# Attention by pairs of heads in plain fp32, in a kernel of attention and two feed-forward layers

## The chip, the cores and the metric

The kernel runs on one core of one Trainium2 chip. The number that counts is the device time of one execution, in microseconds (us): the median of three runs before the change is 675.22 us (674.95 to 675.29). Five engines work side by side, each through its own queue in a fixed order: TensorE (PE, the matmuls; PEld is its loading of stationary operands), VectorE (DVE), ScalarE (ACT), GpSimd (POOL) and SyncE (SP, which issues the transfers).

## What is computed

Attention with a window and sinks, then two feed-forward layers, on 2 x 768 = 1536 tokens, 8 heads of 64 dimensions, model width 512, hidden width 2048:

```python
scores = (q @ k.T) / sqrt(64)                  # per batch and head, 768 x 768
keep   = (col < n_sink) | ((row - col >= 0) & (row - col < window))   # n_sink 4, window 128
a      = softmax(where(keep, scores, -1e9));   x = a @ v
h = relu(x @ w_in);  y = (h * h) @ w_out       # first layer
h = y @ w_in2;  g = (a0 + a1 h + a2 h^2 + a3 h^3) / (1 + |b0||h| + |b1| h^2 + 1e-6)
out = g @ w_out2                               # second layer
```

Only scores within 128 positions, and those of the first few columns, count. So a block of 128 queries needs its own block of keys, the block before it, and the first 32 columns (the sinks).

## The kernel before, in words

**Units and groups.** The tokens are cut into four groups (`GROUPS`): group 0 has 512 tokens (two segments of two query blocks), groups 1 and 2 have 256 (one segment), group 3 has 512 (two). A unit of attention is one head of one segment, that is two query blocks: 48 units, 16 of them in segments that begin a sequence ("first" segments: their blocks need 128 and 256 key columns) and 32 in later ones ("later" segments: 288 columns for each block, previous, sinks and own). By group: 16 units (8 first, 8 later) in group 0, 8 later ones in group 1, 8 first ones in group 2, 16 later ones in group 3.

**Steps of a unit** (`att_unit`, a generator whose `yield`s are ticks): scores on PE (line 305) into a PSUM bank, mask, minimum and row statistic on DVE (309), exponential and row sum on ACT (311), reciprocal (315, 316) and normalising (318) on DVE or POOL, transposes on PE (334 for the window, 338 for the 32 sink columns), copies out of PSUM (339, 341), value matmuls on PE (359 for the sinks, 368 for the window), and the evacuation into x (376, 384 and after).

**Two ways to be exact.** The feed-forward matmuls split each fp32 operand into a high and a low part in a rounded format (fp32r) and add three products (lines 447 to 449, 470 to 474, 505 to 507). The attention does the same in "split" units: k and v are split (282, 284, 290, 291), q is stacked as high part over low part on the 128 rows (283, 285), and the probabilities are split on their way out of PSUM (339, 347, 349). In group 0, `PAT = "ppps"` makes three of four units "plain": the matmuls take fp32 operands as they are. The fourth, which is always a later one, is plain for the values and split for the scores. A plain score matmul finds k and q twice on the 128 rows, and q is scaled by half (277).

**What sets the order.** The loop before the first layer runs the 16 units of group 0, one new unit every four ticks. Then `group(g)` runs the two matmul stages of the first layer for group g, and in `slot` it lets attention ticks of the next groups in between (`NUNIT[g]` units, four ticks each). What attention of group g+1 is left at the end of group g runs alone (`while done < gdone[g + 1]`). A scheduler orders the instructions of each engine by a model of time; in groups 1 and 2 (`PINNED`) PE keeps the order of the code. Attention has PSUM banks 2, 3, 6, 7 and 1 ahead of the first layer, 6 and 7 while a group of 512 tokens is in work, and 2, 3, 6 and 7 beside a group of 256. From group 3 on no attention is left, and the second layer follows.

Of the kernel before, what the change touches and what calls it, by code (L numbers as in the profile page):

```python
# [19 lines left out]
P = 128  # L20
# [19 lines left out]
NUNIT = (8, 12, 12)  # L40
CONV = (6, 10, 14, 18, 46, 50)
PAT = "ppps"
# [10 lines left out]
ST_T = 5  # L53
ST_PV = 2
# [8 lines left out]
def seg_dims(seg):  # L63
    _, blk0, nb = seg
    pv = 1 if blk0 > 0 else 0
    wk = nb * KB + P if pv else nb * P
    wq = nb * P
    nkb = nb + pv
    wv = (nkb + pv) * D
    return wk, wq, nkb, wv  # L70


def units():
    out = []
    for g, segs in enumerate(GROUPS):
        for h in range(H):
            xo = 0
            for seg in segs:
                out.append((g, h, seg, xo))
                xo += seg[2] * P  # L80
    return out


def pack_attention(q, k, v):
    qT = q.transpose(0, 1, 3, 2)
    kT = k.transpose(0, 1, 3, 2)
    parts = []
    for g, h, seg, _ in units():
        b, blk0, nb = seg
        cols = []  # L90
        sk = kT[b, h][:, :NSK]
        if blk0 > 0:
            cols.append(kT[b, h][:, (blk0 - 1) * P : blk0 * P])
        for i in range(nb):
            if blk0 > 0:
                cols.append(sk)
            cols.append(kT[b, h][:, (blk0 + i) * P : (blk0 + i + 1) * P])
        cols.append(qT[b, h][:, blk0 * P : (blk0 + nb) * P])
        kq = np.concatenate(cols, axis=1)
        kq = np.concatenate([kq, kq], axis=0)  # L100
        p0 = blk0 - 1 if blk0 > 0 else blk0
        vs = [v[b, h][j * P : (j + 1) * P] for j in range(p0, blk0 + nb)]
        if blk0 > 0:
            vs.append(np.concatenate([v[b, h][:NSK]] * 4, axis=0))
        vv = np.concatenate(vs, axis=1)
        parts += [kq.reshape(-1), vv.reshape(-1)]
    return np.ascontiguousarray(np.concatenate(parts))
# [43 lines left out]
class Fast:  # L151
# [17 lines left out]
    def setup(self):  # L169
# [38 lines left out]
        self.m2 = c.tile([P, KB + P], F32, name="m2")  # L208
# [4 lines left out]
        v.tensor_scalar(fut, rel, 0.0, BIG, op0=ALU.is_lt, op1=ALU.mult)  # L213
        v.tensor_scalar_add(rel1, rel, 128.0)
        cur, prv = m2[:, KB : KB + P], m2[:, 0:P]
        v.tensor_scalar(cur, rel, win, BIG, op0=ALU.is_ge, op1=ALU.mult)
        v.tensor_tensor(cur, cur, fut, op=ALU.max)
        v.tensor_scalar(out, col, ns, BIG, op0=ALU.is_ge, op1=ALU.mult)
        v.tensor_tensor(m0, cur, out, op=ALU.min)
        v.tensor_scalar(prv, rel1, win, BIG, op0=ALU.is_ge, op1=ALU.mult)  # L220
        v.tensor_tensor(m1[:, 0:P], prv, out, op=ALU.min)
        v.tensor_copy(m1[:, P : 2 * P], cur)
        v.tensor_copy(m2[:, P:KB], out[:, :NSK])
        nu = sum(u[2][2] for u in units())
# [5 lines left out]
    def alt_tags(self, alt):  # L230
        if not alt:
            return [None] * 12
        c = NF - 3 * alt
        return [f"{p}{c + i}_{k}" for i in range(3) for k in range(2) for p in ("whi", "wlo")]

    def att_load(self, u, early, alt):
        nc = self.nc
        wk, wq, nkb, wv = seg_dims(u[2])
# [5 lines left out]
        rv = self.att_tile("rawv", wv, F32, bufs=2, alt=self.alt_tags(alt)[9])  # L244
        off = self.att_off
        self.att_off = off + P * (w + wv)
        a = self.io["att"]
        nc.sync.dma_start(raw, a[off : off + P * w].rearrange("(p w) -> p w", w=w))
        off += P * w
        nc.sync.dma_start(rv, a[off : off + P * wv].rearrange("(p w) -> p w", w=wv))  # L250
        return raw, rv

    def att_tile(self, tag, n, dt=F32R, bufs=1, alt=None):
        if alt:
            return self.wp.tile([P, WH], dt, tag=alt, name=tag)[:, :n]
        return self.att.tile([P, n], dt, tag=tag, name=tag, bufs=bufs)

    def att_unit(self, u, raws, alt):
        nc = self.nc
        tags = self.alt_tags(alt)  # L260
        V, A, G = nc.vector, nc.scalar, nc.gpsimd
        g, h, seg, xo = u
        mode = PAT[self.unit_i % len(PAT)] if g == 0 else "b"
        self.unit_i += 1
        plain, plain_pv = mode == "p", mode in "ps"
        b, blk0, nb = seg
        wk, wq, nkb, wv = seg_dims(seg)
        pv = nkb - nb
        n = nb * P
        at = self.att  # L270
        raw, vr = raws
        kr, qr = raw[:, :wk], raw[:, wk:]
        vr3 = vr.rearrange("p (j d) -> p j d", d=D)
        qst = self.att_tile("qst", wq, F32 if plain else F32R, alt=tags[2])
        if plain:
            ks = [kr]
            V.tensor_scalar_mul(qst, qr, -0.0625)
        else:
            khi = self.att_tile("khi", wk, alt=tags[0])
            klo = self.att_tile("klo", wk, alt=tags[1])  # L280
            ks = [khi, klo]
            V.tensor_copy(khi, kr)
            A.mul(qst, qr, -0.125)
            G.tensor_tensor(klo, kr, khi.bitcast(F32), op=ALU.subtract)  # L284
            V.scalar_tensor_tensor(qst[64:128], in0=qr[64:128], scalar=-0.125,
                                   in1=qst[64:128].bitcast(F32), op0=ALU.mult, op1=ALU.subtract)
        yield
        if not plain_pv:
            vst = self.att_tile("vst", (nkb + pv) * 2 * D, alt=tags[3]).rearrange("p (j d) -> p j d", d=2 * D)
            A.copy(vst[:, :, 0:D], vr3)  # L290
            G.tensor_tensor(vst[:, :, D : 2 * D], vr3, vst[:, :, 0:D].bitcast(F32), op=ALU.subtract)
        yield
        ps, sums = [], self.const.tile([P, 4], F32, tag="sums", name="sums", bufs=6)
        for i in range(nb):
            blk = blk0 + i
            if pv:
                off, w, m = i * KB, KB + P, self.m2
# [4 lines left out]
            sc = self.att_bank()  # L302
            ql = qst[:, i * P : (i + 1) * P]
            for j, kk in enumerate(ks):
                nc.tensor.matmul(sc[:, :w], ql, kk[:, off : off + w], start=(j == 0), stop=(j == len(ks) - 1))  # L305
            pt = self.att_tile("p", KB + P, F32, bufs=4, alt=tags[4 + i])
            mn = self.mn[:, self.mn_i : self.mn_i + 1]
            self.mn_i += 1
            self.lastV = V.tensor_tensor_reduce(pt[:, :w], sc[:, :w], m, scale=1.0, scalar=3.0e38,  # L309
                                                op0=ALU.add, op1=ALU.min, accum_out=mn)  # L310
            self.lastA = A.activation(pt[:, :w], pt[:, :w], AF.Exp, scale=-1.0, bias=mn,  # L311
                         accum_out=sums[:, i : i + 1])
            ps.append((pt, w, blk))
            yield
        V.tensor_scalar_add(sums[:, :nb], sums[:, :nb], 1e-9)
        V.reciprocal(sums[:, :nb], sums[:, :nb])
        for i, (pt, w, blk) in enumerate(ps):
            (G if g in NORM_POOL else V).tensor_scalar(pt[:, :w], pt[:, :w], sums[:, i : i + 1], 0.0,
                                               op0=ALU.mult, op1=ALU.add)
# [683 lines left out]
```

## Time and profile before

| | us |
|---|---|
| median of 3 runs | 675.22 |
| the profiled execution | 675.02 |
| its span, first to last instruction | 673.2 |
| PE busy in the span | 648.8 |
| DVE busy | 509.0 |
| ACT busy | 475.3 |
| POOL busy | 163.5 |

A matmul's record lasts longer than its turn on PE: records overlap, and the next one starts while the one before it is still leaving the array. What a matmul costs is therefore the distance from its start to the next start, read from a timeline, and not the length of its record. Another habit of the records: a plain fp32 matmul has two records of equal shape, an fp32r matmul and a transpose have one.

### The profile page before, as it was taken

Reading aid. Unit: us, or ns where it says so; the run is one execution under the profiler, and the core shown is the slowest. Engines: PE = TensorE matmul, PEld = TensorE weight load, DVE = VectorE, ACT = ScalarE, POOL = GpSimd, SP = SyncE. Lnnn points to the kernel's source line nnn. Section 1 sums busy time; section 2 is a strip of 40 time slices with the busy share of each in tenths; the row PEclk is TensorE's granted clock in tenths of the full one; section 3 lists DMA queues with packets and bytes.
Section 4 is the critical chain, followed back from the end, with each engine's and each line's share of the span. In section 5 each row is a group of like instructions: output and inputs, shape, how many; then the busy total and the mean of one; then the engine's idle time right before and its main releaser. Section 6 shows DMA issues by size and latency. Waiting matters only on the chain.

```text
span 673.2 us, 10158 instructions
## 1 busy us (share of the span) xinstructions
PE 648.8 (96%) x3433; PEld 543.9 (81%) x3433; DVE 509.0 (76%) x1068; ACT 475.3 (71%) x1044; POOL 163.5 (24%) x174
## 2 busy tenths in 40 slices
PE   5999999999799999999999999999999999999995
PEld 3666788788699999999888888888888888888884
DVE  6976877778678877875666648999788878787772
ACT  4877977777677776776777757878677666666662
POOL 3553111111223332322100001344223333222221
PEclk9999999999799999999999999999999999999998
DMA  7761555555323222210466640000010000000001
GB/s 283 251 204 47 182 173 168 152 174 157 115 88 90 65 85 85 66 36 1 129 190 193 201 132 1 0 1 0 1 56 8 1 0 1 31 32 1 0 1 68
DMA packets 25403, 58.41 MB, mean 87 GB/s; under 512 B 3200, under 2 KB 9600, under 8 KB 25344
## 3 DMA queue, kind: packets, MB, share of 16 engines
q1 hardware_dynamic: 24768, 57.55, 26.9%
q8 instruction: 29, 0.48, 0.3%
q14 instruction: 30, 0.25, 0.1%
q10 hardware_dynamic: 576, 0.14, 0.1%
HBM read 54.53 MB, written 3.15 MB: 86 GB/s over the span
## 4 chain that ended last, share of the span: by engine, by line
PE 72%; DVE 0%; ACT 0%; issue 0%
PE b L447 11%; PE b L449 11%; PE b L448 11%; PE b L505 6%; PE b L507 6%; PE b L506 6%; PE b L470 4%; PE b L474 4%; PE b L471 4%; PE b L368 3%; PE b L305 2%; PE b L334 1%; PE b L359 1%; PE b L338 1%; PE b L658 0%
## 5 line engine op out<-in xcount | busy, mean ns | idle before, releaser
L447 PE MATMUL b<-xhi,whi 128*128 128x512 f32 (+1 forms) x320 | 111.5, 353 | 1.1 <-ACT xhi L376 0.8
L448 PE MATMUL b<-xlo,whi 128*128 128x512 f32 (+1 forms) x320 | 111.9, 350 | 0.0
L449 PE MATMUL b<-xhi,wlo 128*128 128x512 f32 (+1 forms) x320 | 111.6, 349 | 0.1
L496 POOL TENSOR_TENSOR glo<-t,ghi 128x512 fp32r<-128x512 f32 x34 | 45.0, 1323 | 213.5 <-ACT ghi L495 195.4
L470 PE MATMUL b<-ghi,whi 128*128 128x512 f32 (+1 forms) x256 | 77.0, 341 | 0.4 <-ACT b L458 0.4
L471 PE MATMUL b<-ghi,wlo 128*128 128x512 f32 (+1 forms) x256 | 76.1, 337 | 0.1
L506 PE MATMUL b<-wlo,ghi 128*128 128x512 f32 x192 | 74.7, 389 | 0.0
L505 PE MATMUL b<-whi,ghi 128*128 128x512 f32 x192 | 74.4, 389 | 0.0
L507 PE MATMUL b<-whi,glo 128*128 128x512 f32 x192 | 71.9, 389 | 0.0
L447 PEld LDWEIGHTS b<-xhi,whi 128*128 128x128 f32 x320 | 60.7, 191 | 8.5 <-ACT xhi L376 1.0
L449 PEld LDWEIGHTS b<-xhi,wlo 128*128 128x128 f32 x320 | 61.0, 191 | 8.0 <-DVE wlo L432 0.5
L448 PEld LDWEIGHTS b<-xlo,whi 128*128 128x128 f32 x320 | 61.0, 191 | 7.3
L284 POOL TENSOR_TENSOR klo<-raw,khi 128x448 fp32r<-128x448 f32 (+1 forms) x32 | 33.4, 1045 | 126.6 <-PE b L305 111.5
L311 ACT ACTIVATE p<-p,mn 128x288 f32<-128x288 f32 (+2 forms) x96 | 48.3, 503 | 19.1 <-DVE mn L309 18.6
L432 DVE TENSOR_TENSOR wlo<-wt,whi 128x512 fp32r<-128x512 f32 x64 | 44.8, 700 | 22.3 <-ACT whi L431 21.9
L431 ACT CAST whi<-wt 128x512 fp32r<-128x512 f32 x64 | 39.5, 617 | 26.9 <-PE b L448 21.0
L474 PE MATMUL b<-glo,whi 128*128 128x512 f32 (+1 forms) x256 | 56.2, 337 | 0.2 <-DVE glo L459 0.2
L309 DVE CUSTOM_DVE_ANT_0 p<-b,m 128x288 f32<-128x288 f32 (+2 forms) x96 | 39.7, 419 | 20.8 <-PE b L305 19.7
L129 DVE SCALAR_TENSOR_TENSOR wt<-st,top 128x512 int32<-128x512 int32 x64 | 48.1, 752 | 6.5 <-ACT top L128 4.4
L471 PEld LDWEIGHTS b<-ghi,wlo 128*128 128x128 f32 x256 | 48.0, 189 | 5.1 <-DVE wlo L432 0.5
L470 PEld LDWEIGHTS b<-ghi,whi 128*128 128x128 f32 x256 | 47.8, 189 | 5.1 <-ACT b L458 0.6
L128 ACT CAST top<-st 128x512 f16<-128x512 bf16 x64 | 49.6, 775 | 1.2 <-DVE wt L129 1.1
(151 smaller groups left out, 1549.3 us busy)
## 6 DMA issues: line engine op xcount, KB each, us to landing
st<-w SPq DMA_DIRECT2D x64, 512.0 KB, 3.9
raw<-att SPq DMA_DIRECT2D x24, 352.0 KB, 2.9
rawv<-att SPq DMA_DIRECT2D x32, 128.0 KB, 2.3
raw<-att SPq DMA_DIRECT2D x12, 256.0 KB, 3.5
raw_e<-att SPq DMA_DIRECT2D x8, 352.0 KB, 5.3
out<-o SPq DMA_DIRECT2D x8, 256.0 KB, 2.3
rawv<-att SPq DMA_DIRECT2D x16, 64.0 KB, 2.6
raw_e<-att SPq DMA_DIRECT2D x4, 256.0 KB, 5.5
```

Of the source, the lines that this page charges most:

```text
L128: nc.scalar.copy(top.bitcast(F16).rearrange("p (n w) -> p n w", w=2)[:, :, 1], head)
L129: nc.vector.scalar_tensor_tensor(t.bitcast(I32), in0=mid, scalar=13, in1=top, op0=ALU.logical_shift_right, op1=ALU.bitwise_or)
L311: self.lastA = A.activation(pt[:, :w], pt[:, :w], AF.Exp, scale=-1.0, bias=mn, accum_out=sums[:, i : i + 1])
L447: nc.tensor.matmul(h[:, :n], whi[:, cs], xhi[:, c, :n], start=(c == 0), stop=False)
L448: nc.tensor.matmul(h[:, :n], whi[:, cs], xlo[:, c, :n], start=False, stop=False)
L449: nc.tensor.matmul(h[:, :n], wlo[:, cs], xhi[:, c, :n], start=False, stop=(c == NC - 1))
L470: nc.tensor.matmul(acc[m], whi[:, ms], ghi, start=(f == 0 and not pk), stop=pk, **kw)
L471: nc.tensor.matmul(acc[m], wlo[:, ms], ghi, start=False, stop=pk, **kw)
L474: nc.tensor.matmul(acc[m], whi[:, ms], glo, start=False, stop=pk or f == NF - 1, **kw)
L505: nc.tensor.matmul(acc[t], ghi[:, ts_], whi, start=(f == 0), stop=False)
L506: nc.tensor.matmul(acc[t], ghi[:, ts_], wlo, start=False, stop=False)
L507: nc.tensor.matmul(acc[t], glo[:, ts_], whi, start=False, stop=(f == NF - 1))
```

## The change

A unit becomes a pair of heads of one segment, 24 units in place of 48, and all of it is plain fp32. The loads bring k and q of the first head on partitions 0 to 63 and of the second on 64 to 127, without doubling, so a score matmul of one head uses 64 of the 128 rows of the array, and the two heads write two PSUM banks. The scale goes into the mask step. No operand of the attention is split or scaled any more: lines 277, 282 to 285, 290, 291, 347 and 349 have no successor. The window's probabilities are transposed as before, one bank for each head; one goes out by ACT, the other by DVE. The sinks of both blocks (64 columns that lie side by side) are transposed by a plain fp32 matmul against the identity, 64 columns wide, each head into its half of the partitions of one bank. The value matmuls are 64 columns wide, one head on either column half of the array, and both heads leave in one copy of 128 partitions; the sinks' values come as a third load, laid out with zeros around them, so that one moving operand serves both heads. Half of the normalising of every unit (block 0) is POOL's. A unit has seven ticks instead of ten (in group 0: of fourteen), and still a new one starts every four; the ticks at which the first weights are converted, and the units per group, are halved with the units.

In the diff the lines taken out of `att_unit` are left away, as are the masks (sign turned), the packing on the host, the loads and the second program for other inputs.

```diff
 PINNED = (1, 2)
-NUNIT = (8, 12, 12)
-CONV = (6, 10, 14, 18, 46, 50)
-PAT = "ppps"
+NUNIT = (4, 4, 8)
+CONV = (3, 7, 11, 15, 23, 27)
+PER = 4
...
-ST_T = 5
-ST_PV = 2
+ST_T = 1
+ST_PV = 1
...
 def seg_dims(seg):
     _, blk0, nb = seg
     pv = 1 if blk0 > 0 else 0
-    wk = nb * KB + P if pv else nb * P
+    wk = 2 * nb * P + NSK if pv else nb * P
     wq = nb * P
     nkb = nb + pv
-    wv = (nkb + pv) * D
-    return wk, wq, nkb, wv
+    return wk, wq, nkb, nkb * P, (2 * nb * D if pv else 0)
...
     def att_unit(self, u, raws, alt):
         nc = self.nc
         tags = self.alt_tags(alt)
         V, A, G = nc.vector, nc.scalar, nc.gpsimd
...
+        g, c, seg, xo = u
         b, blk0, nb = seg
...
+        wk, wq, nkb, wv, wsk = seg_dims(seg)
         pv = nkb - nb
         n = nb * P
...
+        raw, vr = raws[:2]
         kr, qr = raw[:, :wk], raw[:, wk:]
...
+        rows = [slice(D * k, D * k + D) for k in range(2)]
+        wp_ = KB + P
+        pt = self.att.tile([P, 2, nb, wp_], F32, tag="p", name="p", bufs=2)
+        sums = self.const.tile([P, 4], F32, tag="sums", name="sums", bufs=6)
+        ws = []
         for i in range(nb):
             blk = blk0 + i
             if pv:
...
+                off, w, m = 2 * i * P, KB + P, self.m2[:, (1 - i) * NSK :][:, : KB + P]
             elif i == 0:
                 off, w, m = 0, P, self.m0
             else:
                 off, w, m = (i - 1) * P, 2 * P, self.m1
...
+            ws.append(w)
+            sc = [self.att_bank() for _ in range(2)]
+            for k, r in enumerate(rows):
+                nc.tensor.matmul(sc[k][:, :w], qr[r, i * P : (i + 1) * P], kr[r, off : off + w],
+                                 start=True, stop=True)
+            for k in range(2):
+                mn = self.mn[:, self.mn_i : self.mn_i + 1]
+                self.mn_i += 1
+                p = pt[:, k, i, :w]
+                self.lastV = V.tensor_tensor_reduce(p, sc[k][:, :w], m, scale=-0.125, scalar=3.0e38,
+                                                    op0=ALU.add, op1=ALU.min, accum_out=mn)
+                self.lastA = A.activation(p, p, AF.Exp, scale=-1.0, bias=mn,
+                                          accum_out=sums[:, k * nb + i : k * nb + i + 1])
             yield
...
+        V.tensor_scalar_add(sums[:, : 2 * nb], sums[:, : 2 * nb], 1e-9)
+        V.reciprocal(sums[:, : 2 * nb], sums[:, : 2 * nb])
+        for i in range(nb):
+            for k in range(2):
+                p = pt[:, k, i, : ws[i]]
+                (G if i in NORM_POOL else V).tensor_scalar(p, p, sums[:, k * nb + i : k * nb + i + 1], 0.0,
+                                                           op0=ALU.mult, op1=ALU.add)
         yield
         for _ in range(ST_T if g == 0 else 1):
             yield
...
+        nk = 2 * nb - (0 if pv else 1)
+        pT = []
+        for k in range(2):
+            pieces = []
+            for i in range(nb):
+                e = ws[i] - (NSK if pv and i == 0 else 0)
+                if blk0 + i > 0:
+                    pieces.append(pt[:, k, i, e - 2 * P : e - P])
+                pieces.append(pt[:, k, i, e - P : e])
+            tb = self.att_bank()
+            for j in range(nk):
+                nc.tensor.transpose(tb[:, j * P : (j + 1) * P], pieces[j], self.ident)
+            t = self.att_tile(f"pT{k}", nk * P, alt=tags[k])
+            (A.copy if k == 0 else V.tensor_copy)(t, tb[:, : nk * P])
+            pT.append(t)
+        ob = self.att_bank()
         if pv:
...
+            for k, r in enumerate(rows):
+                both = pt[:, k].rearrange("p i w -> p (i w)")
+                nc.tensor.matmul(ob[r, n : n + P], both[:, 2 * P : 2 * KB], self.ident, start=True, stop=True,
+                                 skip_group_check=True)
+            ps = self.att_tile("pS", P, alt=tags[2])
+            A.copy(ps, ob[:, n : n + P])
         yield
         for _ in range(ST_PV):
             yield
...
+        vr3 = vr.rearrange("p (j d) -> p j d", d=D)
+        o = [ob[r, :n] for r in rows]
+        if pv:
+            sv = raws[2].rearrange("p (j d) -> p j d", d=D)
+            for i in range(nb):
+                for k in range(2):
+                    nc.tensor.matmul(o[k][:, i * P : (i + 1) * P], sv[:, k * nb + i], ps,
+                                     start=i == 0, stop=False, skip_group_check=True)
         jobs, pos = [], 0
         if pv:
...
             jobs.append((0, 0, 1, 0))
             pos = 1
         for i in range(nb):
             wdt = 2 if i + 1 < nb else 1
             jobs.append((i + pv, pos, wdt, i))
             pos += wdt
...
+        for j, (vi, pp, wdt, qi) in enumerate(jobs):
+            for k in range(2):
+                nc.tensor.matmul(o[k][:, qi * P : (qi + wdt) * P], vr3[:, 2 * vi + k],
+                                 pT[k][:, pp * P : (pp + wdt) * P], start=not pv and j == 0,
+                                 stop=j == len(jobs) - 1, skip_group_check=True)
         xs = slice(xo, xo + n)
...
+        if g == 0:
             xhi, xlo = self.x[g]
...
+            A.copy(xhi[:, c, xs], ob[:, :n])
+            V.tensor_tensor(xlo[:, c, xs], ob[:, :n], xhi[:, c, xs].bitcast(F32), op=ALU.subtract)
         else:
...
+            A.copy(self.x32[g][:, c, xs], ob[:, :n])
```

The next rows are PE's order around three places, of before and of the change. In a row stand the line, the operation, what it writes and reads, and the output's size (partitions x elements); b is a PSUM bank, p the probabilities, pT their transpose.

PE beside a group of 256 tokens (group 1's matmuls), a unit of group 3 at its transposes, before:

```order
L448 MATMUL b_2983<-xlo,whi 128x256
L449 MATMUL b_2983<-xhi,wlo 128x256
L334 MATMUL b_3004<-ident,p 128x128 x4
L338 MATMUL b_3009<-ident,p 32x128 x2
L305 MATMUL b_3018<-khi,qst 128x288
L305 MATMUL b_3018<-klo,qst 128x288
L470 MATMUL b_2247<-ghi,whi 128x256
L471 MATMUL b_2247<-ghi,wlo 128x256
```

The same step of a unit of group 3 in the change, beside group 2's matmuls (L295 the scores, L327 and L335 the transposes, L427 to L429 and L450 to L454 the two stages of the first layer):

```order
L429 MATMUL b_2712<-xhi,wlo 128x256
L295 MATMUL b_2733<-raw 128x288
L295 MATMUL b_2734<-raw 128x288
L327 MATMUL b_2741<-ident,p 128x128 x4
L327 MATMUL b_2748<-ident,p 128x128 x4
L335 MATMUL b_2755<-ident,p 64x128 x2
L450 MATMUL b_2512<-ghi,whi 128x256
L451 MATMUL b_2512<-ghi,wlo 128x256
```

Transposes and scores of one head stood between full-array matmuls; now two score matmuls on 64 rows each, eight transposes and two sink matmuls of 64 columns follow each other.

PE in group 0's matmuls, the scores of one block of a later segment, before:

```order
L474 MATMUL b_1088<-glo,whi 128x512
L474 MATMUL b_1089<-glo,whi 128x512
L305 MATMUL b_1082<-khi,qst 128x288
L305 MATMUL b_1082<-klo,qst 128x288
L359 MATMUL b_1156<-pst,vst 128x256
L368 MATMUL b_1156<-pthi,vst 128x128
```

The change, the first head of a block (bank b_778), and further on the second head of it (b_779):

```order
L450 MATMUL b_804<-ghi,whi 128x512
L451 MATMUL b_804<-ghi,wlo 128x512
L295 MATMUL b_778<-raw 128x288
L454 MATMUL b_802<-glo,whi 128x512
L454 MATMUL b_803<-glo,whi 128x512
```

```order
L451 MATMUL b_801<-ghi,wlo 128x512
L450 MATMUL b_802<-ghi,whi 128x512
L295 MATMUL b_779<-raw 128x288
L451 MATMUL b_802<-ghi,wlo 128x512
L450 MATMUL b_803<-ghi,whi 128x512
```

The two halves of one block, which the code issues together, are 79 rows apart here; each stands alone between matmuls of the whole array.

PE from group 0 to group 1, before (from the last matmul of group 0 on):

```order
L474 MATMUL b_1091<-glo,whi 128x512
L368 MATMUL b_2033<-pthi,vst 128x256
L368 MATMUL b_2033<-pthi,vst 128x128
L305 MATMUL b_1974<-khi,qst 128x256
L305 MATMUL b_1974<-klo,qst 128x256
L368 MATMUL b_2033<-ptlo,vst 128x256
L368 MATMUL b_2033<-ptlo,vst 128x128
L305 MATMUL b_2131<-khi,qst 128x256
L305 MATMUL b_2131<-klo,qst 128x256
L305 MATMUL b_2065<-khi,qst 128x128
L305 MATMUL b_2065<-klo,qst 128x128
L334 MATMUL b_2057<-ident,p 128x128 x3
```

The change, at the end of group 0:

```order
L428 MATMUL b_1645<-xlo,whi 128x256
L429 MATMUL b_1645<-xhi,wlo 128x256
L295 MATMUL b_1511<-raw 128x256
L427 MATMUL b_1645<-xhi,whi 128x256
L428 MATMUL b_1645<-xlo,whi 128x256
L429 MATMUL b_1645<-xhi,wlo 128x256
L295 MATMUL b_1666<-raw 128x128
L295 MATMUL b_1667<-raw 128x128
L327 MATMUL b_1674<-ident,p 128x128 x3
L327 MATMUL b_1680<-ident,p 128x128 x3
L427 MATMUL b_1691<-xhi,whi 128x256
```

Before, eight value matmuls, six score matmuls and three transposes stand alone between group 0's last matmul, the first row, and the next matmuls of group 1 (b_2162; the last four of the value matmuls are below the piece). In the change the last value matmuls of group 1's own attention stand further up, inside group 0's last matmuls; three score matmuls and six transposes stand between matmuls of group 1 (b_1645 and b_1691).

## Rows read from the trace of the kernel before

**Rows 1.** The page: span, and busy time of each engine.

```profile
span 673.2 us, 10158 instructions
...
PE 648.8 (96%) x3433; PEld 543.9 (81%) x3433; DVE 509.0 (76%) x1068; ACT 475.3 (71%) x1044; POOL 163.5 (24%) x174
```

**Rows 2.** Five stages: us, busy us of PE, PEld, DVE, ACT, POOL; PEclk; DMA, GB/s.

```profile
0.00:70.55 70.55, 60.04 (x299) 40.44 (x300) 52.59 (x194) 49.69 (x143) 30.30 (x52) 1.00 0.58 194
70.55:183.46 112.91, 107.62 (x527) 87.79 (x527) 85.61 (x194) 87.76 (x198) 16.23 (x19) 0.97 0.52 162
183.46:254.07 70.61, 69.47 (x569) 67.19 (x568) 57.38 (x176) 52.23 (x163) 20.34 (x24) 1.00 0.27 80
254.07:315.70 61.63, 61.63 (x495) 58.76 (x495) 43.77 (x125) 40.26 (x118) 14.88 (x16) 1.00 0.17 51
315.70:673.20 357.50, 350.04 (x1551) 289.69 (x1548) 269.65 (x384) 245.36 (x426) 81.76 (x64) 0.99 0.15 49
```

**Rows 3.** PE's longest wait in all: total us, times, longest.

```profile
PE b L305 <- DVE qst L277: 6.3, 2, 4.8
```

**Rows 4.** Timeline of PE in group 1's matmuls, split units: start, us, instruction.

```profile
222.52 0.61 PE L334 MATMUL b<-ident,p 128*128 128x128 f32 x4
...
223.11 0.38 PE L305 MATMUL b<-khi,qst 128*128 128x288 f32 x1
...
223.46 0.28 PE L447 MATMUL b<-xhi,whi 128*128 128x256 f32 x1
...
224.88 0.30 PE L305 MATMUL b<-khi,qst 128*128 128x288 f32 x1
...
225.15 0.28 PE L470 MATMUL b<-ghi,whi 128*128 128x256 f32 x1
...
226.09 0.64 PE L474 MATMUL b<-glo,whi 128*128 128x256 f32 x4
226.66 0.38 PE L359 MATMUL b<-pst,vst 64*128 64x256 f32 x1
...
227.71 0.33 PE L447 MATMUL b<-xhi,whi 128*128 128x256 f32 x1
```

**Rows 5.** The same view in group 0's attention, plain units.

```profile
47.12 0.55 PE L334 MATMUL b<-ident,p 128*128 128x128 f32 x3
47.50 1.14 PE L305 MATMUL b<-raw_e,qst 128*128 128x288 f32 x4
48.57 0.86 PE L368 MATMUL b<-pthi,rawv 128*64 128x256 f32 x4
...
49.59 0.60 PE L334 MATMUL b<-ident,p 128*128 128x128 f32 x4
50.03 1.23 PE L305 MATMUL b<-raw_e,qst 128*128 128x256 f32 x4
51.19 0.64 PE L359 MATMUL b<-pst,rawv 32*64 32x256 f32 x2
...
52.77 0.44 PE L334 MATMUL b<-ident,p 128*128 128x128 f32 x2
```

**Rows 6.** The same view from group 0 to group 1; idle time before in brackets.

```profile
169.82 0.34 PE L368 MATMUL b<-ptlo,vst 128*128 128x256 f32 x2
172.74 0.39 PE L305 MATMUL b<-khi,qst 128*128 128x256 f32 x1 [2.58 <-DVE qst L285]
...
177.99 0.52 PE L447 MATMUL b<-xhi,whi 128*128 128x256 f32 x1
...
180.65 0.59 PE L334 MATMUL b<-ident,p 128*128 128x128 f32 x3
180.99 0.31 PE L305 MATMUL b<-khi,qst 128*128 128x128 f32 x1
...
182.97 0.34 PE L368 MATMUL b<-pthi,vst 128*128 128x256 f32 x2
...
183.46 0.62 PE L658 MATMUL b<-zero 128*128 128x128 bf16 x8
```

More of the change, by code (lines that the diff above doesn't have):

```diff
@@ L75, in units @@
     for g, segs in enumerate(GROUPS):
-        for h in range(H):
+        for c in range(NC):
             xo = 0
             for seg in segs:
-                out.append((g, h, seg, xo))
+                out.append((g, c, seg, xo))
                 xo += seg[2] * P
@@ L87, in pack_attention @@
     parts = []
-    for g, h, seg, _ in units():
+    for g, c, seg, _ in units():
         b, blk0, nb = seg
[L90 to L94, printed above, removed]
-            if blk0 > 0:
[L96 to L106, printed above, removed]
+        kq, vv, sinks = [], [], []
+        for half in range(2):
+            h = 2 * c + half
+            kb = [kT[b, h][:, j * P : (j + 1) * P] for j in range(NBLK)]
+            if blk0 > 0:
+                cols = [kb[blk0 - 1], kb[blk0], kT[b, h][:, :NSK], kb[blk0], kb[blk0 + 1]]
+            else:
+                cols = kb[:nb]
+            cols.append(qT[b, h][:, blk0 * P : (blk0 + nb) * P])
+            kq.append(np.concatenate(cols, axis=1))
+            p0 = blk0 - 1 if blk0 > 0 else blk0
+            vv.append([v[b, h][j * P : (j + 1) * P] for j in range(p0, blk0 + nb)])
+            for i in range(nb if blk0 > 0 else 0):
+                z = np.zeros((P, D), v.dtype)
+                r = NSK * (half * nb + i)
+                z[r : r + NSK] = v[b, h][:NSK]
+                sinks.append(z)
+        kq = np.concatenate(kq, axis=0)
+        parts += [kq.reshape(-1), np.concatenate([x for pair in zip(*vv) for x in pair], axis=1).reshape(-1)]
+        if sinks:
+            parts.append(np.concatenate(sinks, axis=1).reshape(-1))
     return np.ascontiguousarray(np.concatenate(parts))
@@ L301, in att_unit @@
                 off, w, m = (i - 1) * P, 2 * P, self.m1
[L302 to L310, printed above, removed]
@@ L844, in segments @@
                 pv = 1 if blk0 > 0 else 0
-                k0 = P + i * KB + NSK if pv else i * P
+                k0 = P + i * (KB + P) if pv else i * P
                 q0 = wk + i * P
-                v0 = (i + pv) * D
-                out[(b, h, blk0 + i)] = (kq, vv, k0, q0, v0)
+                for half in range(2):
+                    r0 = half * D
+                    v0 = (i + pv) * P + r0
+                    out[(b, 2 * c + half, blk0 + i)] = (kq[r0 : r0 + D], vv, k0, q0, v0)
         return out
```

158 lines of the change are left out of this document (35 added, 123 removed).

## The prediction

> **What bounds the kernel now.** I read the page first, then a table of five stages, PE's waits, and the timeline of PE where attention and matmuls mix. PE is busy 648.8 of 673.2 us; no other engine is over 76% [rows 1]. The stages show where it is not: 10.5 us are idle in the first (70.55 less 60.04: the attention of group 0 ahead of the matmuls), 5.3 in the second (group 0's matmuls), 1.1 in the third, nothing in the fourth, and the last 357.5 us have no attention and do not change [rows 2]. In the second stage the granted clock is 0.97, so PE ran at 1.2 GHz instead of 2.4 for about 6% of 112.91 us, which costs half of that, 3.4 us [rows 2]. The idle time and the slow stretch lie in one place, the passage from group 0 to group 1: after 169.82 PE waits 2.58 us for q's split, later matmuls of attention come in drops, and the stream of group 1 resumes only at 177.99 [rows 6]. So the question is what the attention costs in turns of PE, and what becomes of that passage.
>
> **Prices.** Twelve matmuls of 256 columns in fp32r take 223.46 to 224.88, 0.12 us each; the two of a split score block (288 columns) 0.27 [rows 4]. Four transposes take 0.44, 0.11 each; the four records of two plain score matmuls of 288 columns take 47.50 to 48.57, and without the change of shape behind them 0.96, 0.24 each [rows 5]. That is two cycles a column in each of two records, so a record of 128 columns is 0.11 and one of 256 0.22. A stay on part of the array costs extra: the 64-row matmul starts at 226.66 where the four before it end at 226.57 (0.09) [rows 4]; the transposes behind a 64-column stay take 0.38 for three instead of 0.33 [rows 5]. I count 0.09 and 0.05 on entering and again on leaving, 0.3 a stay.
>
> **Before, by those prices.** Split unit of a later segment: transposes and a score block 0.94 (222.52 to 223.46), the other block 0.27, sinks and values 226.57 to 227.71 and 0.05, together 2.40 [rows 4]; two heads 4.80. Split unit of a first segment: transposes 0.34, scores 0.54 (180.99 to 182.97 less twelve matmuls), values 0.49: 1.37 [rows 6], two heads 2.74. Plain ones in group 0: scores 0.96, transposes 0.44 and 0.22, sinks and values 51.19 to 52.77 with their entry, 3.3; with split scores 2.9; first segments 1.85 (48.57 to 49.59 holds values and sink transposes) [rows 5]. Two heads of both segments: 3.3 + 2.9 + 2 x 1.85 = 9.9, four times that 39.6.
>
> **After, part by part.** A pair of a later segment has 8 score records of 0.24, 8 transposes of 0.11, 4 sink records of 0.11, 16 value records of 0.11 and 4 of 0.22, and 4 stays (two of scores, sinks, values). What no row of before shows is two matmuls on different halves of the array at once. One end: they run one behind the other, as every row does: 1.92 + 0.88 + 0.44 + 2.64 + 1.2 = 7.08. The nearest rows say no more than that a matmul on fewer rows is not cheaper alone: the 32-row sink matmul of 51.19 has two full records [rows 5]. The other end: the halves run fully side by side. I take a value between, nearer to the second: records keep their order, a head's second record needs its own half, but the other head's first one does not, so of four records in a row the two in the middle lie together. The rows allow it: what paces PE in them is the stream of columns, and each half has its own partitions, its own columns, and for scores its own bank. Then scores take 1.44, sinks 0.33, values 1.37, and the pair 5.22. A first segment: 0.99 + 0.66 + 0.70 + 0.9 = 3.25, end to end 4.20.
>
> The Trainium skill, TensorEngine Tiling (Array Packing), Key Properties, says that tiles work independently and can load and multiply in parallel; TensorE: Matmul & The Clock Gate, Part 3, says that matmuls still start and end in program order. No row here shows either; by the two together the sum is the one with the middle records overlapped, by the first alone the fully parallel one below.
>
> **Sum over PE's turns** (overlapped | end to end):
> 12 pairs of later segments in groups 1 and 3: 12 x 0.42 = +5.0 | 12 x 2.28 = +27.4.
> 4 pairs of first segments in group 2: 4 x 0.51 = +2.0 | +5.8.
> Group 0: 4 x (5.22 + 3.25) = 33.9, against 39.6: -5.7 | +5.5.
> Halves apart: while only banks 6 and 7 are free, and in part ahead of that, PE's order has 38 score matmuls without their partner beside them, 19 blocks. Each loses its overlap (about 0.2) and adds a stay (0.3, less where another one adjoins, so 0.22): +8.0 | +4.2.
> Together +9.3 | +42.9.
>
> **Waits.** The passage to group 1 had 5.3 us idle (0.9 of it earlier in the stage) and 3.4 by the clock. Its head is q's split (line 285), which is gone, and group 1's last value matmuls now stand inside group 0's stream, so x is ready in time. What is late next is the last exponential of group 2's first pair: in ACT's order it stands behind the four copies of y, and DVE's and POOL's normalising and six transposes wait for it. I leave 2 us: -6.7. The third stage's wait is partly for a subtraction of line 349: -0.6. In the first stage 6.3 us went to q's scaling, 4.8 of them ahead of the first matmul [rows 3], but that wait ends with the first load, and the second with the next; both stay late without the scaling. I keep its 10.5 us, between -5 (the chain of a unit is seven ticks long, not fourteen) and +3 (a pair's row sums wait for four exponentials). All other edits cost nothing as long as PE stays the bound: DVE loses scaling, casts and subtractions and gains one copy of 512 columns a pair, ACT loses the splits, and POOL's normalising (line 318) precedes its transposes by two ticks of 12 to 24 matmuls. If that cover fails, DVE's 52.59 of 70.55 us in the first stage [rows 2] is the first to show. The third load of a later pair goes out with the other two ahead of need; there are 64 attention loads instead of 96.
>
> 675.0 (the profiled execution, 0.2 under the median) + 9.3 - 6.7 - 0.6 = 677.0 us. End to end: 675.0 + 42.9 - 7.3 = 710.6.
>
> **Rivals.**
> Fully side by side, or a shorter start: a score block then takes two records instead of three (29 blocks together, -5.8), sinks and values save another 3.0: 668; with 5 us off the start 663. For it: the halves share nothing in the code. Against it: single records in order are all that the timelines show. It gets 0.22, and is the case that ends faster: it decides as soon as the PE work falls by more than 3 us against my sum.
> No overlap: 710.6. For it: no row shows two matmuls streaming at once. 0.20.
> One kind only: if scores do not overlap, about 5.8 more than my sum, 683; if values and sinks do not, 16 x 1.38 + 8 x 0.62 = 27 more, 704. 0.11.
> The clock: more short stays and transposes could cost PE its 2.4 GHz, as the stretch between 172.74 and 177.99 did [rows 2, 6]; another 7 us at half rate is 3.4 more, 680. 0.05.
> My forecast has 0.42.
>
> **How the numbers follow.** A measurement of this kernel tells 0.2% from no change, about 1.35 us: faster is under 673.9, slower over 676.6. The forecast's own range is 670 to 684 (the first stage's -5 and +3, and 2 us on the stays), of which I give 0.27 to faster, 0.15 to the same and 0.58 to slower: 0.11, 0.06, 0.25. The parallel case adds 0.19, 0.02 and 0.01, no overlap and one kind 0.31 to slower, the clock mostly slower. Together 0.31, 0.09, 0.60. The range for 8 in 10 runs from 664 (nearly all of the parallel case) to 711 (half of the no-overlap case).
>
> **What would show it.** In the timeline of PE, the second head's first score record starts within a few tens of ns of the first head's second one if I am right, 0.24 behind it if nothing overlaps, beside the first head's first one if all is parallel. Sinks and values of a later pair take 1.4 in one stay, or 2.6. The stage of groups 2 and 3's attention gets longer by about 7 us together, the stage of group 0's matmuls changes little because the added stays eat the saved wait, and its granted clock rises to 1. I am wrong if the first stage, not the pinned ones, carries the difference, if stays cost far from 0.3, or if DVE or ACT become the releaser of PE's waits.

## The result, and the profile after

The changed kernel takes 680.26 us (median of four runs, 678.46 to 681.13) beside 675.25 for the kernel before: a ratio of 1.0071, interval 1.0049 to 1.0093. It is slower, as forecast, and the time lies in the forecast's own range; the forecast was 677.0. The profiled execution took 678.46 us, 3.4 us more than the one before in its span; it is the fastest of the four, so what is read from it accounts for 3.4 of the 5.0 us by which the medians differ. The page's span and busy line, against [rows 1]:

```profile
span 676.6 us, 9626 instructions
...
PE 656.2 (97%) x3521; PEld 522.7 (77%) x3521; DVE 421.3 (62%) x849; ACT 423.4 (63%) x912; POOL 113.9 (17%) x122
```

DVE, ACT and POOL have 88, 52 and 50 us less to do, which brings nothing, because PE is the bound in both. The stages, cut at the same events as [rows 2], with the last one ending at the last matmul:

```profile
0.00:68.37 68.37, 58.86 (x305) 34.27 (x305) 45.21 (x167) 40.17 (x116) 12.25 (x28) 1.00 0.52 178
68.37:180.58 112.21, 110.58 (x549) 82.47 (x547) 59.32 (x129) 74.79 (x160) 5.53 (x8) 0.98 0.43 144
180.58:244.26 63.68, 63.68 (x524) 56.90 (x523) 22.95 (x82) 32.31 (x104) 4.67 (x10) 1.00 0.15 45
244.26:310.04 65.78, 65.78 (x559) 55.33 (x557) 25.39 (x88) 32.02 (x102) 6.67 (x12) 1.00 0.18 53
310.04:666.91 356.87, 356.87 (x1594) 293.69 (x1592) 268.04 (x385) 243.44 (x431) 84.77 (x64) 1.00 0.13 47
```

The beginning of the last stage comes 5.7 us earlier than before (310.04 against 315.70). From there to the end it is 366.6 us (676.6 less 310.04), against 357.5. About 4.3 of these 9.1 us are work that moved behind the cut: 24 second-product matmuls of 256 columns, and the sinks and values of the last pair, 1.46 us (an estimate, with 0.12 us a matmul). The other 4.8 are new, and more than the whole loss of 3.4. (For the same reason the third and fourth stage can't be compared one by one.)

**Two halves at once.** A score block of two heads, then one head's block alone, then sinks and values of a pair; each row gives a start, the time that its records cover, and their number:

```profile
263.45 0.28 PE L429 MATMUL b<-xhi,wlo 128*128 128x256 f32 x1
263.66 0.76 PE L295 MATMUL b<-raw 64*128 64x288 f32 x4
264.35 0.77 PE L327 MATMUL b<-ident,p 128*128 128x128 f32 x5
...
73.94 0.39 PE L429 MATMUL b<-xhi,wlo 128*128 128x512 f32 x1
74.26 0.75 PE L295 MATMUL b<-raw 64*128 64x288 f32 x2
74.94 0.50 PE L450 MATMUL b<-ghi,whi 128*128 128x512 f32 x1
...
269.68 0.66 PE L348 MATMUL b<-pS,raws 128*64 128x128 f32 x8
270.17 1.04 PE L360 MATMUL b<-pT,rawv 128*64 128x128 f32 x12
271.14 0.38 PE L450 MATMUL b<-ghi,whi 128*128 128x256 f32 x1
```

Four records of two heads take 0.69 us (263.66 to 264.35), two records of one head 0.68 (74.26 to 74.94): the second head is free. But each record takes 0.34 and not the 0.24 of [rows 5]. With 0.1 us to enter (263.45 to 263.66 where a 256-column product has 0.12) and 0.1 to leave, a stay of scores costs about 0.88 us, for one head as for two. Eight sink records and twelve value records take 1.46 together, where their columns end to end would be 16 x 0.107 + 4 x 0.213 = 2.6; here nothing is added to a record.

The Trainium skill (TensorEngine Tiling (Array Packing), Key Properties) has tiles load and multiply in parallel; the equal 0.69 and 0.68 agree. For the 0.1 that a score record has on top, the skill's TensorE: Matmul & The Clock Gate, Part 3, The mechanism, offers a rule: weights are loaded beside a running matmul only where the rows differ, and a head's two records share theirs. The score records agree. The records of sinks and values stand on all rows, so that by the rule they should pay it too, and they don't (eight sink records, four on either half, take 0.49 with their entry), nor do the plain score records on 128 rows, 0.24 each [rows 5]: there the measurement decides, and what costs a record on 64 rows its 0.1 stays open.

**The second layer slows down.** PE alone, 80 us in each of the second layer's three parts, the kernel before and then the changed one:

```profile
400.00:480.00 80.00, 80.00 (x355) 1.00 0.00 1
480.00:560.00 80.00, 80.00 (x355) 1.00 0.04 14
560.00:640.00 80.00, 80.00 (x355) 1.00 0.04 14
```

```profile
400.00:480.00 80.00, 80.00 (x349) 1.00 0.00 1
480.00:560.00 80.00, 80.00 (x355) 1.00 0.04 14
560.00:640.00 80.00, 80.00 (x350) 1.00 0.04 14
```

Same instructions, no idle time, full clock, and yet 6 and 5 matmuls fewer in the first and third part. Where one matmul that reads yhi or ylo follows another, the starts are 0.23 and 0.24 apart by turns, 0.233 on average in the trace, instead of 0.227:

```profile
430.07 0.39 PE L429 MATMUL b<-yhi,wlo 128*128 128x512 f32 x1
430.30 0.40 PE L427 MATMUL b<-yhi,whi 128*128 128x512 f32 x1
430.54 0.39 PE L428 MATMUL b<-ylo,whi 128*128 128x512 f32 x1
430.77 0.40 PE L429 MATMUL b<-yhi,wlo 128*128 128x512 f32 x1
```

11 x 0.227 in 160 us is 2.7 us over the 174 us that these two parts last. They stream yhi and ylo (384 matmuls), tiles at the right end of the memory; the middle part streams xhi and xlo at the left end, where the weights are too. The change made a mask 128 bytes a partition larger, and every left tile behind it moved by 128 bytes; the right ones stayed. Before, yhi, ylo and the weights began at the same address modulo 512; now yhi and ylo lie 128 bytes from the weights, while xhi and xlo moved along with them.

**The end.** From the last matmul's start to the end of the span it is 9.7 us (666.91 to 676.6), against 7.85 (665.35 to 673.2). The last transfer is issued 1.3 us behind that matmul in both (668.19, and 666.63 before), and no engine computes after it. What is longer there stays open. It is no accident of one execution: every kernel below that is built from the changed one has a tail of 9.4 to 10.2 us, and the kernel before with other addresses has 7.8.

### The profile page after: what moved, and what is told of

Read it like the earlier page. It is cut to its first block, busy times and chain, and to the rows that moved or that the text cites. A ratio compares the mean times of both kernels' runs of the same rounds, so it can differ in the third digit from the quotient of the medians.

```text
span 676.6 us, 9626 instructions
## 1 busy us (share of the span) xinstructions
PE 656.2 (97%) x3521; PEld 522.7 (77%) x3521; DVE 421.3 (62%) x849; ACT 423.4 (63%) x912; POOL 113.9 (17%) x122
## 4 chain that ended last, share of the span: by engine, by line
PE 94%; ACT 2%; DVE 1%; DMA 1%; issue 0%; POOL 0%
PE b L427 14%; PE b L429 13%; PE b L428 13%; PE b L450 7%; PE b L451 7%; PE b L454 7%; PE b L486 6%; PE b L485 6%; PE b L487 6%; PE b L295 5%; PE b L327 3%; PE b L360 3%; PE b L348 1%; PE b L335 1%; ACT p L303 1%; DMA ab<-a 1%
## 5 line engine op out<-in xcount | busy, mean ns | idle before, releaser
L427 PE MATMUL b<-xhi,whi 128*128 128x512 f32 (+1 forms) x320 | 112.8, 357 | 0.3 <-ACT xhi L366 0.3
L429 PE MATMUL b<-xhi,wlo 128*128 128x512 f32 (+1 forms) x320 | 111.5, 349 | 0.0
L476 POOL TENSOR_TENSOR glo<-t,ghi 128x512 fp32r<-128x512 f32 x34 | 47.7, 1402 | 228.4 <-ACT ghi L475 117.3
L450 PE MATMUL b<-ghi,whi 128*128 128x512 f32 (+1 forms) x256 | 84.1, 345 | 0.0
L301 DVE CUSTOM_DVE_ANT_0 p<-b,m 128x288 f32<-128x288 f32 (+2 forms) x96 | 38.3, 420 | 72.9 <-PE b L295 70.8
L451 PE MATMUL b<-ghi,wlo 128*128 128x512 f32 (+1 forms) x256 | 83.0, 341 | 0.0
L486 PE MATMUL b<-wlo,ghi 128*128 128x512 f32 x192 | 74.8, 390 | 0.0
L311 POOL TENSOR_SCALAR p<-p,sums 128x288 f32<-128x288 f32 (+1 forms) x48 | 27.4, 582 | 273.4 <-DVE sums L307 85.2
L427 PEld LDWEIGHTS b<-xhi,whi 128*128 128x128 f32 x320 | 60.5, 190 | 15.0 <-issue 6.8
L487 PE MATMUL b<-whi,glo 128*128 128x512 f32 x192 | 68.4, 389 | 0.0
L429 PEld LDWEIGHTS b<-xhi,wlo 128*128 128x128 f32 x320 | 60.9, 190 | 7.7 <-issue 0.4
L436 ACT ACTIVATE b<-b 128x512 f32<-128x512 f32 (+1 forms) x64 | 30.7, 481 | 53.7 <-PE b L429 53.3
L439 DVE TENSOR_TENSOR glo<-b,ghi 128x512 fp32r<-128x512 f32 (+1 forms) x64 | 35.5, 554 | 41.2 <-ACT b L438 40.2
L454 PE MATMUL b<-glo,whi 128*128 128x512 f32 (+1 forms) x256 | 55.8, 338 | 0.0
L450 PEld LDWEIGHTS b<-ghi,whi 128*128 128x128 f32 x256 | 48.4, 189 | 8.1 <-issue 3.1
```

The source lines that it names most:

```text
L427: nc.tensor.matmul(h[:, :n], whi[:, cs], xhi[:, c, :n], start=(c == 0), stop=False)
L429: nc.tensor.matmul(h[:, :n], wlo[:, cs], xhi[:, c, :n], start=False, stop=(c == NC - 1))
L450: nc.tensor.matmul(acc[m], whi[:, ms], ghi, start=(f == 0 and not pk), stop=pk, **kw)
L451: nc.tensor.matmul(acc[m], wlo[:, ms], ghi, start=False, stop=pk, **kw)
L454: nc.tensor.matmul(acc[m], whi[:, ms], glo, start=False, stop=pk or f == NF - 1, **kw)
L476: self.lastL = nc.gpsimd.tensor_tensor(glo, t3, ghi.bitcast(F32), op=ALU.subtract)
```

## The experiments

**Addresses.** The changed kernel without its pad tile, with an order of PE that is the same to the instruction:

```diff
-        c.tile([P, PAD // 4], F32, name="pad")
```

> The changed kernel without its 128-byte pad tile, which puts every left-side tile back at the addresses of the kernel before (the mask grew by 128 bytes); PE's order is the same. Theory A (addresses): the second layer's 512-column matmuls on yhi and ylo go back from 229 and 238 ns to 227, 480 of them in two of its three parts by 2 to 4 ns on average beside 192 others, about 3.9 us; the median falls from 680.3 to about 676. Rival B (the pace comes from the changed order of the two layers, or from the chip's clock): no change, 680.3 and the same alternation.

Measured: 677.76 us, ratio to the kernel before 1.0013 (0.9997 to 1.0029), 2.5 us less by the medians and 3.9 by the ratios. Its twelve executions fall into two groups, five from 673.5 to 675.5 us (the profiled one, 673.46, is the fastest) and seven from 677.7 to 678.6. The profiled execution has the old pace back:

```profile
400.00:480.00 80.00, 80.00 (x354) 1.00 0.00 1
480.00:560.00 80.00, 80.00 (x354) 1.00 0.04 14
560.00:640.00 80.00, 80.00 (x355) 1.00 0.04 14
```

The other way round, on the kernel before:

```diff
-PAD = 128
+PAD = 256
```

> The kernel before with a pad of 256 bytes instead of 128: the same order, every left-side tile 128 bytes further, yhi and ylo where they were. Theory A (addresses): its second layer takes the pace of the changed kernel's, 230 ns a matmul in the first and third part, and it gets about 4 us slower, 679. Rival B: 675.3.

Measured: 678.69 beside 675.99, ratio 1.0040 (1.0026 to 1.0055), 2.7 us, and the slow pace appears in the same two parts of an otherwise untouched kernel:

```profile
400.00:480.00 80.00, 80.00 (x349) 1.00 0.00 1
480.00:560.00 80.00, 80.00 (x355) 1.00 0.04 14
560.00:640.00 80.00, 80.00 (x350) 1.00 0.04 14
```

The profiled executions of the changed kernel and of the first run are 5.0 us apart, and most of what is beyond 2.7 is chance: PE's order is the same, and the clock fell at the passage for 3.4 us in the one, which costs 1.7, and not in the other. And half the shift, on the changed kernel (`PAD = 64`):

> The changed kernel with a pad of 64 bytes instead of 128: the left tiles stand 64 bytes further than in the kernel before, the right ones where they were. If any difference of the addresses modulo 512 is enough, the second layer's first and third part show 229 and 238 ns again (mean 230); if only a whole 128 bytes count or the left tiles' own place, 227, or another mean.

One run, 676.74; the slow pace is there (349, 355 and 349 matmuls). So theory A holds, with 2.7 us in place of my 3.9: what counts is where the streamed tile lies against the tiles of the weights, since the middle part, whose tiles all moved together, keeps its pace. 64 bytes off are as bad as 128 (0.233 us in the trace), and equal is good. Which distance matters beyond that was not tried.

**Stays.** Each of a block's two score matmuls is made to wait for the readers of both banks:

```diff
+                if nb_[1 - k] in self.rd:
+                    self.tc.add_manual_dep(mm.ins, self.rd[nb_[1 - k]].ins.name, ...)
```

> The changed kernel in which either score matmul of a block also waits for the other head's bank to be read, so that both become ready together: PE's order has 8 score matmuls without a partner beside them instead of 32. Theory C (a stay for one head costs as much as a stay for two: 0.88 us by the trace, 0.09 to enter, 0.35 and 0.33 for the records, 0.11 to leave): 12 stays less, 12 x 0.88 = 10.5 us less of PE, from 680.3 to about 670, less what the later start of the first head costs. Rival D (my price, 0.42 a block apart): -5.0, about 675. Rival E (the wait for both banks delays the units by as much): 680 or more.

Measured: 673.0, ratio 0.9956 (0.9941 to 0.9971). PE is busy 646.1 us instead of 656.2, and PE's order has 49 stays instead of 60: 10.1 / 11 = 0.92 each. At an equal clock it is about 1.0 (an estimate), since more of this execution ran at half rate: the granted clock was 0.86 from 40 to 70 us. PE's idle time ahead of the last matmul grew from 11.1 to 16.7 us, and all of it lies in the first 70:

```profile
0.00:40.00 40.00, 29.07 (x166) 17.48 (x168) 28.59 (x112) 24.56 (x71) 7.67 (x22) 1.00 0.72 248
40.00:70.00 30.00, 24.27 (x148) 15.14 (x145) 19.81 (x62) 20.00 (x54) 4.56 (x7) 0.86 0.34 108
```

Busy time of score records of 288 columns from later loads, the changed kernel, this one, and the next:

```profile
L295 PE MATMUL b<-raw 64*128 64x288 f32 x96 | 24.1, 455 | 0.0
```

```profile
L296 PE MATMUL b<-raw 64*128 64x288 f32 x96 | 20.4, 455 | 2.2 <-ACT pT L336 2.2
```

```profile
L295 PE MATMUL b<-raw 64*128 64x288 f32 x96 | 35.1, 455 | 1.0 <-DVE mn L300 0.6 <-ACT x L368 0.5
```

The same 96 records, each as long in every run (455 ns), cover 20.4, 24.1 or 35.1 us of PE, by how many of them lie beside another. The third kernel is the opposite test, a tick between the two heads of every block:

```diff
+            for k, r in enumerate(rows):
+                sc = self.att_bank()
...
+                yield
```

> The changed kernel with the two heads' score blocks in different ticks everywhere: PE's order has 69 single score matmuls and 27 in runs, against 32 and 64. Theory C: some 18 more stays at 0.88 us, +16, about 696. Rival D: 18 x 0.42 = +7.6, about 688. If halves that stand together gained nothing at all: +18 x 0.2 (a stay's entry and exit alone), 684. On top of each, units that are two or four ticks longer may add waits.

Measured: 689.98, ratio 1.0208 (1.0193 to 1.0223); PE busy 668.3, 12.1 more with 79 stays instead of 60: 0.64 each, between the two theories; that the blocks of first segments with 128 and 256 columns are shorter may be why. Dearer than my 0.42 in either direction.

**By turns or head by head.** The loop of the values (that of the sinks is turned round in the same way):

```diff
-        for j, (vi, pp, wdt, qi) in enumerate(jobs):
-            for k in range(2):
+        for k in range(2):
+            for j, (vi, pp, wdt, qi) in enumerate(jobs):
```

> The changed kernel with the sinks and the values of one head ahead of those of the other, instead of by turns, so that only one record at each seam has a partner on the other column half. If two halves really multiply at once: 128 columns are 0.107 us a record and 256 columns 0.213 in either kernel, by turns half of them are free; 288 records of 128 and 96 of 256 columns take 51 us end to end, 33 in the trace of the changed kernel, less two seams a pair: +15 us, 695. If a record alone also pays its weights' load, as a score record of 288 columns does (0.347 instead of 0.24), up to 384 x 0.1 / 2 = 19 more, 714. If the starts 6 ns apart are only how the profiler writes them down: no change, 680.

Measured: 686.87, ratio 1.0158 (1.0142 to 1.0174). My 695 was wrong: the same pair of a later segment now reads

```profile
272.51 0.66 PE L348 MATMUL b<-pS,raws 128*64 128x128 f32 x8
273.00 1.30 PE L360 MATMUL b<-pT,rawv 128*64 128x128 f32 x12
274.24 0.39 PE L450 MATMUL b<-ghi,whi 128*128 128x256 f32 x1
```

The sinks take 0.49 as before, though head 0's four records now stand ahead of head 1's; the values take 1.24 instead of 0.97, and not the 1.7 of one behind the other. So PE starts the other half's work though two matmuls of the first half stand in front of it. About 0.27 a pair, some 4 us in 16 pairs, is the order's (a pair of a first segment takes 0.81 instead of 0.80). The medians differ by 6.6; what the other 2 to 3 us are was not separated. The profiled execution, 693.68 us and the slowest of the five, lost more by the clock, which was 0.50 from 47.4 to 74.8 us:

```profile
47.40:74.80 27.40, 27.40 (x94) 15.59 (x93) 10.74 (x33) 9.26 (x27) 1.92 (x4) 0.50 0.17 54
```

PE was hardly idle in that stretch, and 63 of its 94 records were scores, sinks and values on half arrays. What made the clock fall was not separated.

**Both repairs.** No pad, both heads made ready together, and the values one tick behind the transposes (`ST_PV = 0`), so that no score block is queued in between: 44 stays.

> The changed kernel without the pad, with both heads of a block made ready together, and with the values one tick behind the transposes instead of two, so that no score block is queued between a unit's transposes and its values: 44 stays of scores in PE's order instead of 60. By theory C (0.88 us a stay) and theory A (3.9 us of addresses): 680.3 - 16 x 0.88 - 3.9 = 662, plus the some 5 us of waits that the pairing brought in the first stage of the run before, about 667. By my old price of 0.42: 680.3 - 6.7 - 3.9 + 5 = 675. If the values now come too early for the copies that they read, PE waits in the two groups whose order is written out, 0.5 us a unit, +4.

Measured: 665.26, ratio 0.9848 (0.9834 to 0.9862), the fastest of all, 10 us under the kernel before. PE is busy 636.7 against 651.8 of the kernel without the pad: 15.1 / 16 = 0.94 a stay, but the tick has a part in it (below). Its first two stages, and PE's largest waits:

```profile
0.00:70.32 70.32, 50.68 (x305) 31.13 (x305) 49.13 (x173) 44.88 (x125) 12.22 (x28) 1.00 0.58 194
70.32:173.80 103.48, 102.97 (x542) 79.62 (x542) 54.48 (x117) 68.41 (x147) 5.77 (x8) 1.00 0.45 141
```

```profile
PE b L296 <- DVE mn L306: 5.2, 3, 2.2
PE b L296 <- DMA raw<-att: 4.7, 1, 4.7
PE b L458 <- ACT ghi L445: 2.5, 1, 2.5
PE b L334 <- POOL p L317: 2.4, 3, 1.5
```

The first stage has 8.2 us less work and is 2 us longer: there PE is not the bound, and pairing only makes it wait (first row). The gain is in the stage of group 0's matmuls, 103.48 instead of 112.21; 1.1 of these 8.7 us are PE's waits, and 1.7 the clock, which did not fall there. Three more runs take this apart. Pairing only behind the first stage:

> The same, but the two heads are made ready together only behind the first stage, where two banks are left: 52 stays instead of 60. By theories A and C: 680.3 - 8 x 0.88 - 3.9 = 669.4, without the waits of the first stage, so near the run before or up to 3 us behind it: if stays in the first stage lie beside waits anyway, the two are equal; if they are paid in full, this one is 2 us slower.

Measured: 674.83, ratio 0.9971 (0.9954 to 0.9989), a miss. Again there are two groups: five of twelve executions from 670.5 to 673.1 us, seven from 674.7 to 675.8, the profiled one among them. Its clock rose late: its products of 512 columns still follow each other by 0.43 us at 33 us into the run (1.2 GHz),

```profile
32.76 0.63 PE L436 MATMUL b<-xlo,whi 128*128 128x512 f32 x1
33.19 0.63 PE L437 MATMUL b<-xhi,wlo 128*128 128x512 f32 x1
```

where those of the changed kernel have 0.23 at 29.5 us:

```profile
29.57 0.40 PE L429 MATMUL b<-xhi,wlo 128*128 128x512 f32 x1
29.81 0.39 PE L428 MATMUL b<-xlo,whi 128*128 128x512 f32 x1
```

The trace has the rise at 34.7 us, at 22.3 in the changed kernel. (The clock column of a stage row reads 1.00 ahead of the rise; the records' pace shows it.) PE was busy for 12.1 of these 12.4 us, and half of that is 6: without it 674.8 would be 668.8, near the 669.4. That the executions near 670.5 had an earlier rise is likely, as the profiled one of the run without the pad, which is in its lower group, had it at 21.8; it is not shown, since only one of each kernel was profiled. The tick alone, without the pairing:

> The changed kernel without the pad and with the values one tick behind the transposes, but with the heads' score blocks left as they were: 60 stays, as in the changed kernel. If the stays carry the gain of the run with 44 of them, this one is equal to the changed kernel without the pad, 674 to 678. If the tick itself carries it (values and copies of a unit closer together), it is near 669 or below.

Measured: 674.57 (670.47 to 676.16), ratio 0.9967 (0.9949 to 0.9985). Against the 1.0013 of the kernel without the pad that is 3.1 us less, and the intervals do not touch: with the same 60 stays the tick alone is worth about 3 us, though the profiled execution had its clock rise only at 34.8 us. So neither theory is whole. The 0.94 a stay above is too much: take half of what PE did ahead of the rise off its busy time (28.3 us here, 15.8 in the run with 44 stays), and the two kernels are 12.7 us apart, 0.8 for each of 16 stays (an estimate). Last, all divisions by the row sums on DVE:

```diff
-NORM_POOL = (0,)
+NORM_POOL = ()
```

> The kernel of the run with 44 stays, in which VectorE divides both blocks' exponentials by their row sums and GpSimd none. In that run PE waited 2.4 us for GpSimd's division in three places and 5.2 us for VectorE's reductions in three others. If the division's place is what is late: 2.4 us less, 663. If VectorE's turns in the first stage decide (two divisions of 288 more a unit ahead of the next reductions): 665 to 668. If the waits only move: 665.

Measured: 667.51, ratio 0.9873 (0.9857 to 0.9890). GpSimd's wait is gone, that for DVE's reductions is 6.7 us instead of 5.2: it looks as if DVE's turns in the first stage decide, though the intervals of the two kernels touch, and in this profiled execution the clock fell twice for 3.4 us. The division stays better where it was.

## Why the prediction was right or wrong

The side and the range were right, but that the sum came near is luck: its errors, each of 2 to 7 us, stand against each other. One of them is the clock. Either execution ran at 1.2 GHz at two places, at the start and at the passage; PE's busy time in them, before and after:

```profile
0.00:17.00 17.00, 9.72 (x27) 1.00 0.78 284
174.00:180.85 6.85, 5.11 (x20) 0.50 0.30 93
```

```profile
0.00:22.30 22.30, 15.95 (x55) 1.00 0.80 288
175.85:179.30 3.45, 3.45 (x16) 0.51 0.03 5
```

Half of each is what the clock cost. In the profiled executions' +3.4 us:

| | forecast | measured |
|---|---|---|
| PE's waits, all stages | -3.9 | -5.8: 10.5, 5.3 and 1.1 became 9.5, 1.6 and 0 [rows 2] |
| clock of the passage | -3.4 | -0.8 |
| clock at the start | 0 | +3.1 |
| PE's turns at full rate | +9.3 | +2.3, what is left |
| the second layer | 0 | +2.7 |
| behind the last matmul | 0 | +1.9 |

- **The turns** were the worst-sized term: +9.3 against +2.3. By stages it is -4.3 in the first, +3.8 in the second and +2.8 behind (estimates, from PE's busy time less half of what ran at half rate), so the attention of groups 0 and 1 came to -0.5 where the sum had +4.0, dearer halves apart included; which of its prices are too high was not separated. The +2.3 is known to about 1 us: by the same reckoning the kernels without the pad and with half of it come within 0.2 of the change, and the kernel before with the larger pad is 1.2 above the kernel before.
- **The start** had no term. The first stage's clock reads 1.00 in [rows 2], and yet 17 us of it ran at half rate, and 22 in the change. Whether that difference is the change's or chance is not shown: the kernel before with its larger pad had 11.5.
- **The step that failed** in the mechanism is "the last 357.5 us have no attention and do not change". They have no attention, but their tiles stand behind those that the attention made larger. Taking the shift out, and putting it into the kernel before, showed some 2.7 us by itself. I had compared instructions and order, and no addresses.
- **The mechanism of the overlap** was wrong, its size not. I had the middle two of four records overlap, 3 x 0.24 = 0.72 a score block; it is two full overlaps of records that are 0.34 long, 0.69. Of sinks and values I expected 1.4, and 1.46 it is. The rival of no overlap fell, and the side-by-side one was right in mechanism but not in time, since its score records were priced at 0.24.
- **Halves apart** were mis-sized: 0.42 a block, for an overlap and a part of a stay. A head alone costs as much as two, 0.88 by the trace and 0.8 to 1.0 in the runs that took stays away. There were fewer of them than my 19 blocks, though: PE's order has 60 stays for 48 blocks, 12 too many, since heads of different blocks often found each other. 12 x 0.88 is 10.6 us, against 8.0.
- **The passage**: right but for the clock. q's split is gone, and what is late next is what I named, the normalising ahead of the six transposes of group 2's first pair: 1.6 us where I had left 2. But I had the granted clock rise to 1, and it fell there again, to 0.98 over the stage; in the run without the pad, with the same order, it did not.

```profile
PE b L327 <- POOL p L311: 1.6, 1, 1.6
```

- **The pinned groups**: their two stages were to be some 7 us longer. From the end of group 0's matmuls to the first product behind the second layer's gate it is 233.84 us (180.58 to 414.42) against 233.47 (183.46 to 416.93). 1.1 of wait went, and seven products of 512 columns fewer stand in between (1.6 us): about 2.8 for PE, with 0.3 of addresses taken off, where the twelve pairs in it were priced at +5.4.

## What to carry to other kernels

When a matmul fills half of the array, count the stays and not the records: what matters is that the other half's work stands beside it in the order, and that a scheduler which sees two free banks at different moments will pull the two apart. Before calling a stage untouched, compare the addresses of its tiles as well as its instructions; here a table that grew by 128 bytes slowed every product that streams a tile from the other end of the memory. And where two errors of opposite sign meet in a sum, only experiments on each term show it: here the kernel was 10 us under the old one once addresses and stays were mended and the values stood one tick earlier.

## What was not expected of the hardware

The pace of a 512-column matmul depends on where its two operands lie: 0.227 us with the streamed tile and the weights at the same address modulo 512, 0.233 on average with them 64 or 128 bytes apart, with nothing else changed. Matmuls on one half of the array do not hold up those on the other that stand some places behind them: twelve value records in head-by-head order take 1.24 us, in turns 0.97, end to end 1.7. And PE's clock does not rise at the same time in every execution: in the executions profiled here it rose at 11.5 to 34.8 us, and between 22 and 35 us that is some 6 us of the time. The order of the instructions alone does not settle it: the kernel before and the same with a pad of 256 bytes have one order, and the rise came at 17.0 in the one and at 11.5 in the other, so that the same matmul reads

```profile
12.88 0.44 PE L305 MATMUL b<-klo,qst 128*128 128x288 f32 x1
```

```profile
12.74 0.29 PE L305 MATMUL b<-klo,qst 128*128 128x288 f32 x1
```

What sets it stays open.
